# A transformer block on one core: the exponentials of softmax shared between ScalarE and VectorE

## The chip, the cores and the metric

The kernel runs on one core of a Trainium2 chip. The metric is device time in microseconds (us) of one execution. The engines are named as the profile names them: PE (TensorE matmuls), PEld (its weight loads), ACT (ScalarE), DVE (VectorE), POOL (GpSimd) and SP (SyncE, which here issues the DMAs). "Clock" is the mean clock that the throttle granted to TensorE, as a share of full speed. All runs whose times are compared here were in the same (fast) state.

## The reference

One layernorm feeds an attention block and a feed-forward block; both are added to the input. S = 2048 tokens, D = 512, 32 heads of 16 elements, F = 1792, bf16 inputs.

```python
# cut to what matters; shapes reshaped and transposed in the original
def reference(A_x, A_wqkv, A_wo, B_x, B_w1, B_w3, B_w2):
    xn = _layernorm(A_x)
    # A: attention
    q, k, v = split_heads(xn @ wqkv)                 # 32 heads, Dh = 16
    scores = einsum("bhqd,bhkd->bhqk", q, k) * (16 ** -0.5)
    o = einsum("bhqk,bhkd->bhqd", softmax(scores), v) @ wo
    # B: SwiGLU
    h = silu(xn @ w1) * (xn @ w3)
    return A_x + o + h @ w2
```

There are 32 x 2048 x 2048 exponentials, 134 million. They come as 2048 score tiles of 128 keys x 512 queries.

## The kernel before

The kernel is planned while it is built. A small planner walks through time with estimated durations, gives each engine a fixed order of instructions, and turns every "this reads what that wrote" into a semaphore wait. That order is fixed when the program is built, so the estimates decide the order and the chip decides the time.

```python
NU = NQC * NG          # 32 units: 4 blocks of 512 queries x 8 groups of 4 heads
RPU = 4 * NT           # 64 score tiles per unit
NR = NU * RPU          # 2048 score tiles
GW = 3                 # score tiles per exp
...
a_cost = lambda n: 0.113 + 0.000835 * n      # what the planner thinks ScalarE needs
d_cost = lambda n: 0.095 + 0.00104 * n       # and VectorE
```

Three score tiles go into three PSUM banks, and one ScalarE instruction takes the exponential of all three (128x1536). There are two such buffers (banks 0 to 2 and 3 to 5), bank 6 is for all dense work (projections and feed-forward), bank 7 for the sum over keys.

```python
def try_score():
    ...                                       # a free one of the two buffers, or return False
    for i, r in enumerate(rs):                # rs: three score tiles
        b = 3 * buf + i
        mms.append((b, KT[32 * j:32 * j + 32, g, kt * 128:(kt + 1) * 128],
                    QT[32 * j:32 * j + 32, u % 3, :], 32 * j))
    o = P.op("pe", f, reads=rd, writes=wr, dur=0.30, name="S%d" % n)
    ...
    def emit():
        q = P.op("act", lambda e: e.activation(
            PT[:, s0:s0 + w, :].rearrange("p a b -> p (a b)"), ps[:, 3 * buf * 512:(3 * buf + w) * 512],
            ACTF.Exp, scale=SCALE),
            reads=wr, writes=[("PT", r % NSL) for r in rs], dur=a_cost(512 * w))
        ...

def try_pv():                                 # four heads at once, each in its own columns of the array
    ...
    for j in range(4):
        ins = e.matmul(bank(PV)[32 * j:32 * j + 17, :], Vaug[:, kt, 4 * g + j, :],
                       PT[:, (4 * m + j) % NSL, :], start=(kt == 0), stop=(kt == NT - 1),
                       tile_position=(0, 32 * j))
```

The 17th column of `Vaug` is all ones, so the same matmul also gives the denominator of the softmax. A head has 16 elements but stands on 32 rows; the K and Q weights are padded with zeros to that width, so half of each K and Q projection computes zeros:

```python
wk = wko[:, :].rearrange("p (a b) -> p a b", b=32)     # 16 weights, 16 zeros per head
...
elif try_score() or try_pv() or try_dense():           # PE's priorities in the planner
    moved = True
```

## Time and profile before

| | before |
|---|---|
| median time, 3 runs | 1023.9 us (1023.38 to 1024.24) |
| busy: ACT, PE, DVE | 94%, 79%, 20% |
| mean granted clock | 0.824 |
| exps | 683 (all but one of 128x1536), starting every 1.33 us (median) |

First, lines from the profile's page: the span; busy time of each engine in us, as a share of the span, and its instructions; the granted clock in 40 equal slices (9 is 90% or more); the chain of work that ended last, by engine; and the costliest group of instructions (busy us, mean ns of one, then the engine's idle time just before them and what ended most of it).

```profile
span 1022.1 us, 19380 instructions
...
PE 803.3 (79%) x8641; PEld 221.6 (22%) x8641; DVE 203.1 (20%) x347; ACT 959.1 (94%) x755; POOL 61.0 (6%) x81
...
PEclk9999999975579999855559999955558999975578
...
ACT 77%; PE 15%; DVE 3%; DMA 2%; issue 2%; SPq 0%; DVEq 0%
...
L1464 ACT ACTIVATE f_PT<-ps 128x1536 bf16<-128x1536 f32 (+1 forms) x683 | 940.6, 1661 | 24.2 <-PE ps L1454 24.0
```

ScalarE bounds the kernel. It works 94% of the time, the chain runs through it, and before all 683 exps together it waited only 24 us. VectorE is nearly idle: that is what the change wants to use.

One exp lasts 1661 ns, but 683 of them take less time than 683 x 1.66 us would be, because the end of one overlaps the start of the next. The timeline shows it (start, duration, engine, line, operation, how many in a row, and the idle time before):

```profile
457.73 13.68 ACT L1464 ACTIVATE f_PT<-ps 128x1536 bf16<-128x1536 f32 x10
...
464.75 0.61 PE L1454 MATMUL ps<-f_QT,f_KT 32*128 32x512 bf16 x3 [0.20 <-ACT f_PT L1464]
...
466.10 0.61 PE L1454 MATMUL ps<-f_QT,f_KT 32*128 32x512 bf16 x3 [0.20 <-ACT f_PT L1464]
```

Ten exps in 13.68 us: taking one duration off leaves nine distances, (13.68 - 1.66) / 9 = 1.34 us each. This distance from start to start, here called the pitch, and not the duration, is what an exp costs a busy ScalarE. PE's score groups follow in the same step of 1.35 us, each released by an exp.

The table by windows gives, for two stretches: length, busy us (instructions) of PE, PEld, DVE, ACT and POOL, granted clock, DMA share and GB/s.

```profile
150.00:200.00 50.00, 40.44 (x521) 11.90 (x510) 14.93 (x23) 49.19 (x41) 1.26 (x1) 1.00 0.25 30
450.00:500.00 50.00, 37.83 (x244) 7.51 (x248) 2.58 (x5) 49.19 (x37) 1.27 (x1) 0.53 0.16 6
```

ACT is full in both. In the second there is no feed-forward work left for this block of queries, PE runs 244 matmuls in place of 521, and the clock falls to 0.53. PE still looks 76% busy there, because each matmul lasts longer (0.59 us on average, against 0.38 us in the first stretch). Fewer matmuls and a lower clock stand together here; what sets the clock is not shown.

Finally, one line of the groups by form, which matters later: the 16 normalisations of the layernorm on VectorE.

```profile
L1096 DVE TENSOR_SCALAR f_xn_sb<-f_x_sb,f_lnr,f_lnb 128x512 bf16<-128x512 bf16 x16 | 9.4, 630 | 1.2 <-PE ps L1214 0.9 <-POOL f_lnb L1084 0.3
```

### The profile page before, as it was taken

Reading aid. Unit: us, or ns where it says so; the run is one execution under the profiler, and the core shown is the slowest. Engines: PE = TensorE matmul, PEld = TensorE weight load, DVE = VectorE, ACT = ScalarE, POOL = GpSimd, SP = SyncE. Lnnn points to the kernel's source line nnn. Section 1 sums busy time; section 2 is a strip of 40 time slices with the busy share of each in tenths; the row PEclk is TensorE's granted clock in tenths of the full one; section 3 lists DMA queues with packets and bytes.
Section 4 is the critical chain, followed back from the end, with each engine's and each line's share of the span. In section 5 each row is a group of like instructions: output and inputs, shape, how many; then the busy total and the mean of one; then the engine's idle time right before and its main releaser. Section 6 shows DMA issues by size and latency. Waiting matters only on the chain.

```text
span 1022.1 us, 19380 instructions
## 1 busy us (share of the span) xinstructions
PE 803.3 (79%) x8641; PEld 221.6 (22%) x8641; DVE 203.1 (20%) x347; ACT 959.1 (94%) x755; POOL 61.0 (6%) x81
## 2 busy tenths in 40 slices
PE   4987878777799777777789877777779977777795
PEld 2322222221122222111113222211112222211122
DVE  7742233310001222100001222200001122210012
ACT  2799999999999999999999999999999999999991
POOL 5200000000000000000000000000000000000000
PEclk9999999975579999855559999955558999975578
DMA  5402222210111332111111133211101233201112
GB/s 170 89 12 38 38 35 36 22 6 2 6 12 18 58 48 42 23 6 6 6 6 18 35 55 48 38 6 7 5 3 12 38 48 48 33 3 5 6 7 31
DMA packets 80173, 28.88 MB, mean 28 GB/s; under 512 B 70096, under 2 KB 78032, under 8 KB 80080
## 3 DMA queue, kind: packets, MB, share of 16 engines
q1 hardware_dynamic: 80080, 27.54, 21.5%
q8 instruction: 70, 1.15, 0.5%
q14 instruction: 23, 0.19, 0.1%
HBM read 20.71 MB, written 2.10 MB: 22 GB/s over the span
## 4 chain that ended last, share of the span: by engine, by line
ACT 77%; PE 15%; DVE 3%; DMA 2%; issue 2%; SPq 0%; DVEq 0%
ACT f_PT L1464 74%; PE ps L1192 9%; PE ps L1454 4%; ACT f_th L1291 3%; PE ps L1491 2%; DMA f_wv<-in_A_wqkv_dram 1%; DVE f_KT L1203 1%; DMA f_Lc<-f_U 1%; DVE f_hT L1305 0%; DMA f_R<-f_Rrow 0%; DVE f_xn_sb L1096 0%; DVE f_t L1295 0%; PE ps L1214 0%; DVE f_QT L1203 0%; DVE f_osb L1352 0%
## 5 line engine op out<-in xcount | busy, mean ns | idle before, releaser
L1464 ACT ACTIVATE f_PT<-ps 128x1536 bf16<-128x1536 f32 (+1 forms) x683 | 940.6, 1661 | 24.2 <-PE ps L1454 24.0
L1454 PE MATMUL ps<-f_QT,f_KT 32*128 32x512 bf16 x2048 | 319.6, 462 | 139.5 <-ACT f_PT L1464 136.1
L1491 PE MATMUL ps<-f_PT,f_Vaug 128*17 128x512 bf16 x2048 | 239.7, 459 | 0.7 <-DVE f_U L1508 0.7
L1454 PEld LDWEIGHTS ps<-f_QT,f_KT 32*128 32x128 bf16 x2048 | 68.6, 94 | 434.8 <-ACT f_PT L1464 387.9
L1192 PE MATMUL ps<-f_xnT,f_w 128*32 128x512 bf16 x1792 | 129.3, 381 | 38.8 <-DVE f_t L1295 26.6
L1544 POOL TENSOR_TENSOR f_onorm<-f_U,f_R 128x512 bf16<-128x512 f32 x31 | 39.4, 1270 | 908.3 <-DMA f_R<-f_Rrow 749.1
L1491 PEld LDWEIGHTS ps<-f_PT,f_Vaug 128*17 128x17 bf16 x2048 | 50.1, 88 | 156.6 <-issue 148.6
L1508 DVE COPY f_U<-ps 128x512 f32<-128x512 f32 x32 | 22.1, 691 | 241.1 <-PE ps L1491 240.8
L1192 PE MATMUL ps<-f_w,f_hT 128*32 128x512 bf16 x896 | 64.8, 398 | 2.8 <-DVE f_osb L1352 1.6
L1295 DVE SCALAR_TENSOR_TENSOR f_t<-f_th,ps 128x512 f32<-128x512 f32 x56 | 38.5, 687 | 135.2 <-ACT f_th L1291 134.8
L1192 PEld LDWEIGHTS ps<-f_xnT,f_w 128*32 128x32 bf16 x1792 | 42.7, 95 | 86.9 <-issue 61.2
L1305 DVE SCALAR_TENSOR_TENSOR f_hT<-f_t,ps 128x512 bf16<-128x512 f32 x56 | 38.5, 687 | 93.8 <-PE ps L1192 93.8
L1192 PE MATMUL ps<-f_xnT,f_wq 128*32 128x512 bf16 x512 | 47.0, 484 | 7.2 <-DVE f_t L1295 5.6
L1291 ACT ACTIVATE f_th<-ps 128x512 f32<-128x512 f32 x56 | 49.2, 878 | 1.4 <-PE ps L1192 1.4
L1203 DVE CAST f_QT<-ps 128x512 bf16<-128x512 f32 x32 | 22.1, 691 | 127.5 <-PE ps L1192 127.4
L1192 PE MATMUL ps<-f_xnT,f_wko 128*32 128x512 bf16 x512 | 36.5, 389 | 4.7 <-DVE f_t L1295 2.5
L1192 PE MATMUL ps<-f_wo,f_onorm 128*32 128x512 bf16 x512 | 36.7, 388 | 3.5 <-DVE f_onorm L1544 3.5
L1203 DVE CAST f_KT<-ps 128x512 bf16<-128x512 f32 x32 | 22.1, 690 | 45.5 <-PE ps L1192 45.5
L1192 PEld LDWEIGHTS ps<-f_w,f_hT 128*32 128x32 bf16 x896 | 22.3, 98 | 26.8 <-issue 6.6
L1352 DVE TENSOR_TENSOR f_osb<-ps,f_x_sb 128x512 bf16<-128x512 f32 x12 | 8.3, 690 | 84.7 <-PE ps L1192 84.7
L1192 PE MATMUL ps<-f_wv,f_xnT 128*32 128x512 bf16 x256 | 19.7, 443 | 3.8 <-DMA f_wv<-in_A_wqkv_dram 3.5
L1223 ACT ACTIVATE f_xnT<-ps 128x512 bf16<-128x512 bf16 x14 | 7.6, 605 | 15.0 <-PE ps L1214 15.0
(46 smaller groups left out, 137.6 us busy)
## 6 DMA issues: line engine op xcount, KB each, us to landing
f_w<-in_B_w_dram SPq DMA_DIRECT2D x112, 128.0 KB
f_R<-f_Rrow SPq DMA_DIRECT2D x128, 32.0 KB
out_dram<-f_osb SPq DMA_DIRECT2D x16, 128.0 KB
f_w<-in_B_w_dram SPq DMA_DIRECT2D x1, 1792.0 KB
f_x_sb<-in_A_x_dram SPq DMA_DIRECT2D x3, 512.0 KB
f_hT<-in_A_wqkv_dram SPq DMA_DIRECT2D x2, 512.0 KB
f_x_sb<-in_A_x_dram SPq DMA_DIRECT2D x2, 256.0 KB
f_wv<-in_A_wqkv_dram SPq DMA_DIRECT2D x1, 512.0 KB
```

What stands on the lines that cost most here:

```text
L1192: ins = e.matmul(bank(bk)[32 * i:32 * i + 32, 0:ncols], make_lhsT(i), rhs_ap, start=start, stop=stop, tile_position=(0, 32 * i))
L1203: q = P.op("dve", lambda e: e.tensor_copy(dst, src_fn(bk)), reads=[("ps", bk)], writes=[key], dur=d_cost(n))
L1223: q = P.op("act", lambda e: e.activation(xnT[:, :, t * 128:(t + 1) * 128], tb, ACTF.Identity), reads=[("ps", bk)], writes=[("xnT", t)], du ...
L1291: q = P.op("act", lambda e: e.activation(th[:, ss, :], bank(bk), ACTF.Tanh, scale=0.5), reads=[("ps", bk)], writes=[("th", ss)], dur=a_cos ...
L1295: q2 = P.op("dve", lambda e: e.scalar_tensor_tensor(t1[:, ss, :], th[:, ss, :], 1.0, bank(bk), ALU.add, ALU.mult), reads=[("th", ss), ("ps ...
L1305: q = P.op("dve", lambda e: e.scalar_tensor_tensor(hT[:, fc, :], t1[:, ss, :], 0.5, bank(bk), ALU.mult, ALU.mult), reads=[("t1", ss), ("ps ...
L1352: q = P.op("dve", lambda e: e.tensor_tensor(osb[:, ts, :], bank(bk), other, ALU.add), reads=[("ps", bk), ("osum", ts) if part == 2 else (" ...
L1454: ins = e.matmul(bank(b), l_, r_, start=True, stop=True, tile_position=(rp, 0))
L1464: q = P.op("act", lambda e: e.activation(PT[:, s0:s0 + w, :].rearrange("p a b -> p (a b)"), ps[:, 3 * buf * 512:(3 * buf + w) * 512], ACTF ...
L1491: ins = e.matmul(bank(PV)[32 * j:32 * j + 17, :], Vaug[:, kt, 4 * g + j, :], PT[:, (4 * m + j) % NSL, :], start=(kt == 0), stop=(kt == NT ...
L1508: q = P.op("dve", lambda e: e.tensor_copy(U[:, us, :], bank(PV)), reads=[("ps", PV)], writes=[("U", us)], dur=d_cost(512))
L1544: q = P.op(eng, lambda e: e.tensor_tensor(onorm[:, g, :], U[:, us, :], R[:, :], ALU.mult), reads=[("U", us)] + [("R", j_) for j_ in range( ...
```

## The change

The intent is to give part of the exponentials to VectorE, where they are made not by one exp instruction but by arithmetic on bit patterns. The score in PSUM is scaled (through Q) to y = 128 * (s / ln 2 + 127). As a 16-bit integer, y is the bit pattern of a bf16 number: its high bits are the exponent of 2^(s/ln 2), its low seven bits the fraction f. Three bf16 numbers are made from it by 16-bit operations: E = 2^e (the fraction masked away); L * M, where L is the pattern itself, 2^e (1+f), and M = (1+f)/2; and a "shifted chord", the pattern minus 352. Their sum is proportional to 2^(e+f) to about 0.1% (worked out from the formula in the code). The sum is never formed on VectorE: the three terms go through the PV matmul one after another, and PSUM adds them. So a VectorE pair costs PE three times the PV matmuls.

What else changes:

- The exps are pairs (128x1024, two banks) in place of triples: ScalarE has two buffers, banks 0-1 and 2-3, VectorE has banks 4-5.
- The offset 127*128 is added by the score matmul itself: one row of KT holds the constant, the same row of QT holds ones. ScalarE has to take it off again, with a per-partition bias tensor, `act_bias`.
- K and Q heads are no longer padded in the weights. The projection computes two head groups at once, VectorE copies it to a staging tile, and four DMAs per group place the heads on their 32-row strips. Half of the K and Q matmuls fall away.
- The constant rows of KT are filled before the start: two of eight groups on ScalarE, six on GpSimd.
- The buffer of the VectorE terms (`xd`) lies over the tile of x. Its outputs carry the write keys of x, and x is loaded again at the end.

```diff
-    GW = 3
-    NGR = (NR + GW - 1) // GW
-    NSL = 24
+    NPR = 10
+    NON = 11
+    ND = 3
+    YB = 127.0 * 128.0
+    QS = SCALE * 128.0 / math.log(2.0)
+    ASC = math.log(2.0) / 128.0
...
+            e.memset(act_bias[:, :], -127.0 * math.log(2.0) + math.log(KAPPA))
...
+        for g in range(2, NG):
+            P.post("pool", lambda g=g: done.__setitem__(("KTi", g), P.op("pool", lambda e: e.tensor_scalar(
+                KT[:, g, :], sel1[:, 0:1].to_broadcast((128, S)), YB, None, ALU.mult),
+                reads=[("sel1",)], writes=[("KT", g, i) for i in range(NQC)], dur=2.5).end), ready=9.0 + g, prio=3)
...
+                def moves(hh):
+                    for j in range(4):
+                        m = P.dma(lambda e, j=j: e.dma_start(dst(hh)[32 * j:32 * j + 16, :],
+                                                             stg[64 * hh + 16 * j:64 * hh + 16 * j + 16, sl, :]),
...
+                q = P.op("act", lambda e: e.activation(PT[:, s_, :], ps[:, b0 * 512:(b0 + 2) * 512], ACTF.Exp,
+                                                       scale=ASC, bias=act_bias[:, 0:1]),
+                         reads=[("ps", b0), ("ps", b0 + 1), ("abias",)], writes=[("PT", s_)], dur=a_cost(1024))
...
+                q = P.op("dve", lambda e: e.tensor_scalar(yb[:, ys, :], ps[:, 4 * 512:6 * 512], 0.0, 32767.0,
+                                                          ALU.max, ALU.min),
+                         reads=[("ps", 4), ("ps", 5)], writes=[("yb", ys)], dur=1.24)
...
+                def f_e():
+                    q_ = P.op("dve", lambda e: e.tensor_scalar(dsl[:, s_, 0, :], yb[:, ys, :], 0x7F80, None,
+                                                               ALU.bitwise_and),
+                              reads=[("yb", ys)], writes=[("ds", s_, 0)] + XD, dur=0.34)
+                    give(0, q_)
+                def f_m():
+                    P.op("dve", lambda e: e.tensor_scalar(mb[:, ys, :], yb[:, ys, :], 0x7F, 0x3F00,
+                                                          ALU.bitwise_and, ALU.bitwise_or),
+                         reads=[("yb", ys)], writes=[("mb", ys)], dur=0.34)
+                def f_g():
+                    q_ = P.op("dve", lambda e: e.tensor_scalar(dsl[:, s_, 1, :], yb[:, ys, :], -352.0, 0.0,
+                                                               ALU.add, ALU.max),
+                              reads=[("yb", ys)], writes=[("ds", s_, 1)] + XD, dur=0.34)
+                    give(1, q_)
+                def f_t():
+                    q_ = P.op("dve", lambda e: e.tensor_tensor(dsl[:, s_, 2, :].bitcast(BF16),
+                                                               yb[:, ys, :].bitcast(BF16), mb[:, ys, :].bitcast(BF16),
+                                                               ALU.mult),
+                              reads=[("yb", ys), ("mb", ys)], writes=[("ds", s_, 2)] + XD, dur=0.62)
+                    give(2, q_)
...
-                    elif try_score() or try_pv() or try_dense():
+                    elif try_a() or try_d() or try_pv() or try_dense():
```

## The prediction

It was written before the changed kernel had been built or run.

> **What bounds the kernel now.** ScalarE. The busy table has ACT at 959.1 of 1022.1 us (94%), PE 79%, VectorE (DVE) 20%; the chain of waits is 74% ACT exps. In the timeline without feed-forward work (459–471 us), exps of 128x1536 start every 1.345 us though one lasts 1.66 us; a 512-wide tanh costs a pitch of 0.48 us. So a pitch is about 0.06 us + 0.85 ns per column, and 683 exps plus 56 tanhs make about 945 us. The rest is start (about 45 us) and tail. In stages without feed-forward work its granted clock is 0.50–0.57, elsewhere 1.00 (table by windows). [...] the slow windows are those with only 120–130 matmuls per 25 us, against 240 or more.
>
> **What changes.** 1024 pairs (128x1024) replace 683 triples. A pair on ACT should have a pitch of 0.91 us (from the fit). A pair on DVE takes five operations:
> - clamp from PSUM: 128x512 lasts 0.69 us, so 1024 lasts about 1.22;
> - three 16-bit tensor-scalars. [...] The trace's 64-element bf16 ones, 0.174 us alone, 0.09 us pitch, [...];
> - one 16-bit multiply, [...].
>
> Outputs share one set of write keys, so two also wait for the operation before. I estimate 3.1 us per pair; the plan's own table assumes 2.88.
>
> The order is fixed at build time. With its table it balances at about 210 pairs on DVE (190–235).
> - ACT: 814 x 0.91 + 27 = about 770 us.
> - DVE: 210 x 3.1 = 650, plus about 165 of old work (203 now, less half of the K and Q copies) = about 820 us, 90% of the span, from 20%.
> - PE: 256 K and 256 Q matmuls fall away; each DVE pair adds four PV matmuls (about 840); score groups rise from 683 to 1024. At full clock in the timeline a group of four takes 0.22 us; scores to PV and back cost about 0.1 us extra each way (0.32 and 0.31 between starts). So: about 0.4 x 814 + 60 (scores) + 0.22 x 740 (PV) + 0.22 x 992 (dense) = about 770 us.
>
> Removed from the critical path: about 175 us of ACT. Returned: engines stand at 770–820 us of a span near 850, in one fixed order, with only two score buffers for ACT (1.23 + 0.4 us of a 1.83 us round trip, so a PE queue delay over 0.15 us stalls ACT), a DVE running about 8% slower than planned and a start lengthened slightly by packing DMAs. I add about 55 us.
>
> **Predicted: 905 us, range 845 to 975.** Faster by over 2%: 0.93; within 2%: 0.04; slower: 0.03.
>
> **What would show it.** ACT exps 128x1024, about 810, pitch 0.91–1.05 us, ACT busy about 85%; about 210 DVE clamps of 1.2 us; DVE about 90% busy and large in the chain of waits, with PE; [...] granted clock mostly 1.0, mean above 0.92[...]; exps waiting for PE scores for 50–100 us in total against 24 now.
>
> **What would make it wrong.** [...] PE staying at half clock outside feed-forward stages, so that PE bounds (over 950 us); [...] or the fixed order absorbing delays better than I think (850–870 us).

Passages that no trace of this case shows are cut out of it, and the cuts are marked. The prediction put a VectorE pair at 3.1 us, of which the clamp is 1.22. The 3.1, and the 820 us for VectorE made from it, stay as the author's estimate. It can be followed from the planner's durations in the diff (1.24 + 3 x 0.34 + 0.62 = 2.88) and about 0.1 us for each of the two waits.

## The result, and the profile after

The changed kernel takes 969.5 us (median of 4 runs, 966.89 to 971.24) against 1023.64 us (4 runs) for the kernel before. Ratios here and below are the mean time of one kernel's fast runs over that of the other's of the same rounds, so they are not quite the ratios of the quoted medians. This one is 0.9477, 95% interval 0.9444 to 0.951. The change saves 54 us; the prediction said 119. The time lies in the predicted range, near its slow end, but only 54 of the expected 119 us came.

From the page of the kernel after, the lines that answer those of before, and the five operations of a VectorE pair:

```profile
span 968.4 us, 21733 instructions
...
PE 858.6 (89%) x9033; PEld 240.4 (25%) x9033; DVE 878.7 (91%) x1437; ACT 853.9 (88%) x872; POOL 91.4 (9%) x82
...
PEclk9779799999989999999999999999999999999988
...
ACT 43%; DVE 33%; PE 17%; issue 2%; DMA 2%; SPq 2%; DVEq 0%
...
L1550 ACT ACTIVATE f_PT<-ps,f_act_bias 128x1024 bf16<-128x1024 f32 x798 | 819.1, 1153 | 51.3 <-PE ps L1513 44.1
...
L1593 DVE TENSOR_SCALAR f_yb<-ps 128x1024 int16<-128x1024 f32 x226 | 274.4, 1214 | 5.3 <-PE ps L1513 4.9
...
L1627 DVE TENSOR_TENSOR f_xd<-f_yb,f_mb 128x1024 bf16<-128x1024 bf16 x226 | 159.5, 706 | 8.9
...
L1616 DVE TENSOR_SCALAR f_mb<-f_yb 128x1024 int16<-128x1024 int16 x226 | 100.8, 446 | 5.1
L1621 DVE TENSOR_SCALAR f_xd<-f_yb 128x1024 int16<-128x1024 int16 x226 | 98.9, 438 | 7.1
L1610 DVE TENSOR_SCALAR f_xd<-f_yb 128x1024 int16<-128x1024 int16 x226 | 101.3, 448 | 0.0
...
L1134 DVE TENSOR_SCALAR f_xn_sb<-f_xd,f_lnr,f_lnb 128x512 bf16<-128x512 bf16 x16 | 35.3, 2244 | 0.3 <-POOL f_lnb L1122 0.3
```

The planner gave 226 of the 1024 pairs to VectorE. The five operations add up to 274.4 + 159.5 + 100.8 + 98.9 + 101.3 = 734.9 us, 3.25 us per pair if durations are added (one can begin before the last has ended). The clamp that reads PSUM costs 1.21 us; the 16-bit operations are faster, 0.44 us (one input) and 0.71 us (the multiply of two) for the same 1024 elements. The clock is at full speed almost everywhere (mean 0.964). Between 450 and 500 us it is 1.00 with 480 matmuls, where before it was 0.53 with 244; the longest gap between matmuls is as long in both (0.94 and 0.95 us), so that gap does not tell the clock here. And now three engines stand at 88 to 91%, with the chain divided among them. One line stands out: the 16 normalisations take 35.3 us, against 9.4 us before.

Where did the time go? I cut each trace at two points: the start of the exp after the first 2% of all exps (a clamp of VectorE counts as one), and the end of ScalarE's last exp.

| part of the span, us | before | after | difference |
|---|---|---|---|
| start, until 2% of the exps | 54.8 | 81.0 | +26 |
| middle, until the last exp ends | 945.8 | 845.5 | -100 |
| tail | 21.5 | 41.9 | +20 |
| span | 1022.1 | 968.4 | -54 |

So the middle gained 100 us, and nearly half of that was given back at the two ends. The timeline of the kernel after shows each end, and the middle:

```profile
26.77 10.73 POOL L1158 TENSOR_SCALAR f_KT<-f_sel 128x2048 bf16<-128x2048 f32 x2
26.82 10.83 DVE L1134 TENSOR_SCALAR f_xn_sb<-f_xd,f_lnr,f_lnb 128x512 bf16<-128x512 bf16 x2
...
539.29 8.19 ACT L1550 ACTIVATE f_PT<-ps,f_act_bias 128x1024 bf16<-128x1024 f32 x8
...
925.34 1.19 ACT L1550 ACTIVATE f_PT<-ps,f_act_bias 128x1024 bf16<-128x1024 f32 x1
...
931.53 7.57 PE L1216 MATMUL ps<-f_xnT,f_w 128*32 128x512 bf16 x96
...
938.93 3.19 PE L1216 MATMUL ps<-f_w,f_hT 128*32 128x512 bf16 x56
```

- Start: two of GpSimd's fills run from 26.77 to 37.50 us, and two normalisations on VectorE start right after and end with them, at 37.65. Undisturbed, one lasts 0.41 us.
- Middle: eight exps in 8.19 us. Taking off one duration of 1.15, seven distances of 1.006 us remain, not the 0.91 us that the prediction had. The median pitch over the whole trace is 0.997 us.
- Tail: the last exp starts at 925.34, and then PE runs dense matmuls: 469 matmuls start after the last exp ends (336 of the feed-forward, 128 of the attention's output projection), against 177 before (100 and 72).

The middle and the tail as rows of the table by windows:

```profile
75.00:926.00 851.00, 785.27 (x8090) 210.81 (x8082) 803.29 (x1338) 823.02 (x838) 41.63 (x31) 0.98 0.24 31
926.60:968.40 41.80, 28.90 (x469) 12.54 (x469) 12.40 (x24) 1.79 (x3) 0.00 (x0) 0.86 0.20 36
```

and the tail before:

```profile
1000.60:1022.10 21.50, 11.04 (x181) 4.63 (x177) 6.14 (x15) 0.00 (x0) 0.00 (x0) 0.79 0.27 37
```

In the 851 us of the middle ACT is busy 97%, DVE 94% and PE 92%. There is little idle time anywhere, but these shares alone do not tell which engine sets the time. The clamps of VectorE start every 3.78 us on average, at best (the shortest tenth) every 3.12 us.

### The profile page after: what moved, and what is told of

The parts are those of the page before. It is cut to its first block, busy times and chain, and to the rows that moved or that the text cites. A ratio compares the mean times of both kernels' runs of the same rounds, so it can differ in the third digit from the quotient of the medians.

```text
span 968.4 us, 21733 instructions
## 1 busy us (share of the span) xinstructions
PE 858.6 (89%) x9033; PEld 240.4 (25%) x9033; DVE 878.7 (91%) x1437; ACT 853.9 (88%) x872; POOL 91.4 (9%) x82
## 4 chain that ended last, share of the span: by engine, by line
ACT 43%; DVE 33%; PE 17%; issue 2%; DMA 2%; SPq 2%; DVEq 0%
ACT f_PT L1550 42%; DVE f_yb L1593 9%; PE ps L1216 8%; PE ps L1513 5%; DVE f_xd L1627 4%; PE ps L1673 4%; DVE f_xd L1610 3%; DVE f_xd L1621 3%; DVE f_mb L1616 3%; DVE f_xn_sb L1134 3%; DVE f_t L1350 2%; ACT f_th L1346 2%; SPq L1283 1%; DVE f_hT L1360 1%; DMA f_wkv<-in_A_wqkv_dram 1%
## 5 line engine op out<-in xcount | busy, mean ns | idle before, releaser
L1550 ACT ACTIVATE f_PT<-ps,f_act_bias 128x1024 bf16<-128x1024 f32 x798 | 819.1, 1153 | 51.3 <-PE ps L1513 44.1
L1593 DVE TENSOR_SCALAR f_yb<-ps 128x1024 int16<-128x1024 f32 x226 | 274.4, 1214 | 5.3 <-PE ps L1513 4.9
L1673 PE MATMUL ps<-f_xd,f_Vaug 128*17 128x512 bf16 x1356 | 238.7, 388 | 4.5 <-DVE f_xd L1610 2.9
L1216 PE MATMUL ps<-f_xnT,f_w 128*32 128x512 bf16 x1792 | 169.7, 396 | 19.4 <-DVE f_t L1350 13.8
L1627 DVE TENSOR_TENSOR f_xd<-f_yb,f_mb 128x1024 bf16<-128x1024 bf16 x226 | 159.5, 706 | 8.9
L1616 DVE TENSOR_SCALAR f_mb<-f_yb 128x1024 int16<-128x1024 int16 x226 | 100.8, 446 | 5.1
L1621 DVE TENSOR_SCALAR f_xd<-f_yb 128x1024 int16<-128x1024 int16 x226 | 98.9, 438 | 7.1
L1610 DVE TENSOR_SCALAR f_xd<-f_yb 128x1024 int16<-128x1024 int16 x226 | 101.3, 448 | 0.0
L1673 PEld LDWEIGHTS ps<-f_xd,f_Vaug 128*17 128x17 bf16 x1356 | 57.1, 89 | 69.6 <-issue 29.3
L1350 DVE SCALAR_TENSOR_TENSOR f_t<-f_th,ps 128x512 bf16<-128x512 f32 x56 | 38.1, 680 | 7.4 <-ACT f_th L1346 6.8
L1360 DVE SCALAR_TENSOR_TENSOR f_hT<-f_t,ps 128x512 bf16<-128x512 bf16 x56 | 38.1, 681 | 4.1 <-PE ps L1216 2.6
L1134 DVE TENSOR_SCALAR f_xn_sb<-f_xd,f_lnr,f_lnb 128x512 bf16<-128x512 bf16 x16 | 35.3, 2244 | 0.3 <-POOL f_lnb L1122 0.3
```

The source lines that it names most:

```text
L1134: o = P.op("dve", lambda e: e.tensor_scalar(xn_sb[:, xs, :], x_sb[:, t, :], lnr[:, t:t + 1], lnb[:, t:t + 1], ALU.mult, ALU.add), reads=[( ...
L1216: ins = e.matmul(bank(bk)[32 * i:32 * i + 32, 0:ncols], make_lhsT(i), rhs_ap, start=start, stop=stop, tile_position=(0, 32 * i))
L1350: q2 = P.op("dve", lambda e: e.scalar_tensor_tensor(t1[:, ss, :], th[:, ss, :], 1.0, bank(bk), ALU.add, ALU.mult), reads=[("th", ss), ("ps ...
L1550: q = P.op("act", lambda e: e.activation(PT[:, s_, :], ps[:, b0 * 512:(b0 + 2) * 512], ACTF.Exp, scale=ASC, bias=act_bias[:, 0:1]), reads= ...
L1593: q = P.op("dve", lambda e: e.tensor_scalar(yb[:, ys, :], ps[:, 4 * 512:6 * 512], 0.0, 32767.0, ALU.max, ALU.min), reads=[("ps", 4), ("ps" ...
L1610: q_ = P.op("dve", lambda e: e.tensor_scalar(dsl[:, s_, 0, :], yb[:, ys, :], 0x7F80, None, ALU.bitwise_and), reads=[("yb", ys)], writes=[( ...
```

## The experiments

The theories after the result:

- **A**: ScalarE still bounds the middle, so its pitch per pair decides. Against the fit, one exp costs 0.09 us too much; the candidates for that were the bias tensor, the two-level form, the buffers, or a wrong fit.
- **B**: VectorE bounds the middle: 3.78 us per pair times 226 is the 850 us, and ScalarE only waits its turn.
- Beside these, the start is lengthened by GpSimd against VectorE, and PE is short of time because each VectorE pair triples its PV work.

Up to `e8`, the edits are against the kernel after. Differences between experiments are differences of medians, partly from different chips; the kernel before, run beside each of them, had medians of 1022 to 1024 us.

### micro_exp: the pitch of an exp by itself

The kernel does nothing but exps from PSUM (a wrong result), six in a row of each kind.

```python
for w, t in zip(WIDTHS, plain):          # 512 ... 2048 columns
    for r in range(REPS):
        e.activation(t[:, r * w:(r + 1) * w], ps[:, 0:w], ACTF.Exp, scale=0.25)
for r in range(REPS):                    # the same 1024 columns with a bias tensor
    e.activation(bia[:, r * 1024:(r + 1) * 1024], ps[:, 0:1024], ACTF.Exp, scale=0.25, bias=bias[:, 0:1])
# then: alternating bank pairs (alt), and a two-level access pattern (lev)
```

> Wrong result on purpose: no attention, only exps from PSUM on ScalarE, six back to back of each width (512, 768, 896, 1024, 1152, 1280, 1536, 2048 columns), then 1024 columns with a bias tensor, over two bank pairs in turn, and with a two-level pattern. Theory A (pitch is linear in the width, 0.06 us + 0.85 ns per column, as I fitted for the prediction; the 1.005 us pitch in the kernel after is then a wait for PE): start to start 0.48, 0.71, 0.82, 0.91, 1.04, 1.15, 1.345, 1.78 us. Rival B (a 1024-wide exp itself costs 1.005 us, by its shape): 1.00 us for 1024 here too, with no other engine running, and some of the other widths off the line as well. Rival C (the bias tensor costs it): 0.91 without and 1.00 with bias.

| 128 x columns | 512 | 768 | 1024 | 1280 | 1536 | 2048 | 1024 with bias tensor | 1024 alternating banks | 1024 two-level |
|---|---|---|---|---|---|---|---|---|---|
| pitch, us | 0.477 | 0.691 | 0.904 | 1.118 | 1.331 | 1.758 | 0.997 | 0.904 | 0.904 |

The timeline of this kernel, six exps per line:

```profile
53.80 6.68 ACT L54 ACTIVATE bias<-ps,bias 128x1024 bf16<-128x1024 f32 x6
59.78 6.20 ACT L58 ACTIVATE alt<-ps 128x1024 bf16<-128x1024 f32 x6
65.21 6.27 ACT L60 ACTIVATE lev<-ps 128x1024 bf16<-128x1024 f32 x6
```

The first group stands 5.98 us ahead of the second, the second 5.43 us ahead of the third: 0.997 and 0.904 us per exp. The pitch without a bias tensor is 0.051 us + 0.833 ns per column, so the prediction's fit was right, for that form. The bias tensor adds 0.093 us to every exp, and 0.997 is exactly the median pitch of the kernel after. In 798 exps that is 74 us of ScalarE's time. The before kernel had no such operand in its exps, the diff adds one, and the prediction had no term for it.

### e1_fill_act: GpSimd's fills moved to ScalarE

```diff
-            P.post("pool", lambda g=g: done.__setitem__(("KTi", g), P.op("pool", lambda e: e.tensor_scalar(
-                KT[:, g, :], sel1[:, 0:1].to_broadcast((128, S)), YB, None, ALU.mult),
-                ... dur=2.5).end), ready=9.0 + g, prio=3)
+            P.post("act", lambda g=g: done.__setitem__(("KTi", g), P.op("act", lambda e: e.activation(
+                KT[:, g, :], sel1[:, 0:1].to_broadcast((128, S)), ACTF.Identity, scale=YB),
+                ... dur=1.9).end), ready=9.0 + g, prio=3)
```

> The six constant fills of K on GpSimd (5.4 us each in the trace of after) move to ScalarE (1.9 us each), nothing else. Theory: they hold up the normalisations on VectorE (35 us for 16, against 9 us before), and so delay the first steady exps from about 50 to about 75 us. Then the normalisations fall to about 9-12 us, the first clamp on VectorE comes at about 50 us instead of 73, and the time falls by 18-25 us to about 948 us. Rival: the start is long because K and Q now go through a staging tile and DMAs (about 2 us each to land) and because of the single score buffer; then normalisations get shorter but the first clamp stays after 65 us and the time falls by less than 8 us.

Measured: 950.0 us, ratio to before 0.9282 (0.9244 to 0.9321), 19.5 us faster than the kernel after. Groups by form:

```profile
L1134 DVE TENSOR_SCALAR f_xn_sb<-f_xd,f_lnr,f_lnb 128x512 bf16<-128x512 bf16 x16 | 9.4, 631 | 1.0 <-POOL f_lnb L1122 1.0
...
L1158 ACT ACTIVATE f_KT<-f_sel 128x2048 bf16<-128x2048 f32 x6 | 11.2, 1908 | 0.0
```

The normalisations are back at 9.4 us, the first clamp starts at 54.8 us, where it had started at 73.1, and the start by the cut above is 63.3 us (was 81.0). The theory of the start is confirmed for most of it; the start is still 8.5 us longer than before (54.8 us), for which the packing DMAs are a candidate that was not tested. In the trace of the kernel after, two normalisations lasted as long as two fills of 5.37 us (10.83 and 10.73 us). That the fills hold the normalisations up is shown by this run; by what mechanism is not.

### e2_no_d: the new form without VectorE's share

```diff
         def try_d():
             r0 = st["pos"]
-            if r0 >= NR or st["early"] or not idle((4, 5)) or dbuf[0] > P.t:
-                return False
+            return False
```

> VectorE gets no exps; pairs, packing, score buffers as after. Shows what the rest of the change costs before the sharing pays. Theory (exps bound by ScalarE at 1.005 us a pair where three banks cost 1.345 us before): 1024 x 1.005 + 27 + start about 70 + tail 20 = about 1140 us, 11% slower than before, mean granted clock under 0.9 again. Rival (the pitch of 1.005 us comes from PE load or bank conflicts with the VectorE stream): without that stream the pitch falls to about 0.91 us and the time is about 1050 us.

Measured: 1293.42 us, ratio 1.2652 (1.26 to 1.2704), clock 0.716. All 1024 pairs on ScalarE are much slower than either kernel, and slower than expected. One window of it:

```profile
600.00:650.00 50.00, 36.32 (x186) 6.82 (x184) 1.79 (x4) 44.23 (x42) 1.26 (x1) 0.53 0.14 8
```

In 50 us ScalarE gets only 42 instructions through, at clock 0.53; in the timeline two exps start per 2.36 us, 1.18 us each. PE runs 186 matmuls there, and a group of scores lasts 0.61 us, where in the kernel after it takes 0.39 at clock 1.00. Over the run ScalarE waits 139 us before its exps, 96 of them for PV matmuls. As I read it, a PV group stands before the next scores in the fixed order, and two buffers of two banks give ScalarE too little slack for matmuls that long. That the new form by itself (pairs, bias, packing, and only two banks in each of ScalarE's buffers) loses 26% is measured; which of its parts does is not. The sharing wins that back, and more: 1293 to 969.5 us.

### e3_split512: each exp of 1024 as two of 512

```diff
+                def two(e):
+                    for i in range(2):
+                        ins = e.activation(PT[:, s_, 512 * i:512 * i + 512], ps[:, (b0 + i) * 512:(b0 + i + 1) * 512],
+                                           ACTF.Exp, scale=ASC, bias=act_bias[:, 0:1])
+                    return ins
```

> Each exp of 1024 columns on ScalarE is issued as two of 512, one after the other, same plan and order. If 512 columns have a pitch of 0.48 us (as the tanhs do), a pair costs 0.96 instead of 1.005 us, 36 us less ScalarE work: if ScalarE binds the steady stage, 15-35 us faster than after (935-955 us); if VectorE and PE bind it, the time stays within 6 us of after. If the pitch of a pair was a wait for PE, the sum of both halves stays at 1.005 us and nothing changes.

Measured: 1060.01 us, ratio 1.0373 (1.0336 to 1.0411). The halves have a pitch of 0.569 us, 1.14 us per pair, where I had expected 0.48 each. The miss has the same cause as the main one: 0.477 from the table plus 0.093 for the bias is 0.570. The expectation was written before the result of the micro benchmark, which ran in the same series. As ScalarE then has 84% of the chain of waits and the time rises by 90 us, ScalarE's pitch does set the time once it is long enough.

### e4_no_bias: the offset moved to the clamp

Without the constant row the score is 128 s / ln 2, ScalarE needs no bias, and VectorE's clamp, one instruction with two operations, adds the offset itself. The upper clamp is given up; the result was still correct.

```diff
-    YB = 127.0 * 128.0
+    YB = 0.0
+    YD = 127.0 * 128.0 + 128.0 * math.log2(D_SCALE)
...
-                                                       scale=ASC, bias=act_bias[:, 0:1]),
+                                                       scale=ASC),
...
-                q = P.op("dve", lambda e: e.tensor_scalar(yb[:, ys, :], ps[:, 4 * 512:6 * 512], 0.0, 32767.0,
-                                                          ALU.max, ALU.min),
+                q = P.op("dve", lambda e: e.tensor_scalar(yb[:, ys, :], ps[:, 4 * 512:6 * 512], YD, 0.0,
+                                                          ALU.add, ALU.max),
```

> The offset of the bit-pattern exps moves from the K rows and ScalarE's bias tensor into the clamp on VectorE (add, then max, in place of max and min), so that the exps on ScalarE need no bias tensor; plan, order and counts stay those of after. The exp's pitch should fall from 1.005 to 0.91 us where it runs back to back (the measurement of exps alone gave 0.997 with and 0.904 without), so ScalarE has about 74 us less work. Theory A (ScalarE binds the steady stage in after): 35-70 us faster than after, about 900-935 us. Theory B (VectorE and PE, in the fixed order, bind it): 0-20 us faster, ScalarE busy falls to about 80% and its waits for PE grow by what it saves.

Measured: 958.58 us, ratio 0.9376 (0.9342 to 0.941): 11 us faster, though ScalarE lost 47 us of busy time. From the page:

```profile
DVE 68%; PE 19%; issue 5%; DMA 3%; ACT 2%; SPq 2%; DVEq 0%
...
L1551 ACT ACTIVATE f_PT<-ps 128x1024 bf16<-128x1024 f32 x798 | 769.5, 1029 | 83.2 <-PE ps L1514 57.1
```

The shorter exp became a longer wait (83.2 us before the exps, was 51.3), and the chain went from ACT 43% to DVE 68%. For this edit alone theory B holds: behind ScalarE stood VectorE.

### e5_xd: VectorE's outputs without the keys of x

Only the first use of each of the three term buffers has to wait for x; later uses carry the keys of x for nothing. With those keys, an output also waits for the completion of the output before it: in the kernel after, VectorE stood idle for 7.1 and 8.9 us in all before two of the three (lines L1621 and L1627 above).

```diff
-                              reads=[("yb", ys)], writes=[("ds", s_, 0)] + XD, dur=0.34)
+                              reads=[("yb", ys)], writes=[("ds", s_, 0)] + (XD if nd < ND else []), dur=0.34)
```

(The same in the two other outputs.)

> From the fourth VectorE pair on, the three outputs no longer share write keys with the x tile, so that each operation need not wait for the one before to complete. Per pair 3.25 us of busy time should fall to about 2.95-3.05 (two waits of about 0.1 us less), 45-60 us less VectorE work in total. If VectorE binds the steady stage: 20-40 us faster than after. If ScalarE (1.005 us per pair) or PE binds: under 8 us.

Measured: 956.3 us, ratio 0.935 (0.9317 to 0.9384), 13 us faster. The shortest tenth of the clamp's pitch falls from 3.12 to 2.87 us, which is the sum of the planner's own durations (2.88). That is neither of the two expectations (20 to 40 us, or under 8). The two waits are gone, as the page shows, and the chain turns the other way:

```profile
L1627 DVE TENSOR_TENSOR f_xd<-f_yb,f_mb 128x1024 bf16<-128x1024 bf16 x226 | 156.8, 694 | 0.1
...
L1621 DVE TENSOR_SCALAR f_xd<-f_yb 128x1024 int16<-128x1024 int16 x226 | 98.6, 436 | 0.0
...
ACT 69%; PE 13%; DVE 12%; SPq 2%; DMA 2%; issue 1%; DVEq 0%
```

So make VectorE faster and ScalarE is the limit; make ScalarE faster and VectorE is.

### e6_half_d: fewer pairs on VectorE

```diff
             st["dpar"] ^= 2
+            st["dpos"] = r0 + 14
```

> VectorE gets 143 pairs instead of 226, at least seven pairs apart; else as after. ScalarE then has 881 exps. If ScalarE's pitch of 1.005 us binds: 83 more exps are 83 us, partly given back in start and tail: about 1030-1050 us, 6-8% slower than after. If VectorE or PE (83 x 4 fewer PV matmuls, 83 fewer tile-mode switches) bind after, it is not more than 3% slower than after (under 1000 us).

A "tile-mode switch" here is the step from a score group to another group of matmuls and back. In the kernel after, at clock 1.00 (474 to 477 us), a score group and its neighbours start 0.31 to 0.33 us apart, dense and PV groups 0.22 to 0.24.

Measured: 1075.04 us, ratio 1.0533 (1.0475 to 1.0591), clock 0.857, 143 pairs on VectorE and 881 on ScalarE. It is slower than even theory A expected; that the clock fell with the PV work (0.857, against 0.964 in the kernel after) fits this, but was not tested by itself. By this run the planner's share of 226 was not too high.

### e7_three: the three edits together

`e7` is `e1`, `e4` and `e5` in one kernel.

> The three edits together: constant fills on ScalarE, no bias tensor, separate write keys. If the savings add, ScalarE ends at 730+65 us of work and VectorE at about 800, and the time is about 880 us. If PE with its fixed order is the next limit (I estimate about 810 us of PE time with mode switches, plus start and tail), it stays at 905-930 us.

Measured: 912.62 us (909.47 to 913.85), ratio to before 0.8913 (0.8877 to 0.895), and the result is correct. This is the fastest version: 10.9% faster than the kernel before, and 57 us faster than the kernel after. The single savings add up to only 19.5 + 11 + 13 = 43.5 us. From its page:

```profile
PE 836.2 (92%) x9033; PEld 236.2 (26%) x9033; DVE 817.3 (90%) x1437; ACT 810.3 (89%) x878; POOL 59.1 (6%) x76
...
PE 49%; DVE 29%; ACT 14%; DMA 2%; SPq 2%; issue 2%; POOL 0%; DVEq 0%
```

The pitch of the exps is 0.921 us (median), that of the clamps 3.61 us (mean). PE now has the largest part of the chain.

### e8_one_term: a third of the PV work for VectorE's pairs

Its output is wrong, which doesn't matter for the time. Two of the three terms are computed but never summed. If PE's extra work is what limits the kernel after, this must show.

```diff
-                left = [6]
+                left = [2]
...
                               reads=[("yb", ys)], writes=[("ds", s_, 0)] + XD, dur=0.34)
-                    give(0, q_)
```

(The same for `give(1, q_)`, and the counts of tasks per unit.)

> Wrong result on purpose: from after, a VectorE pair still does all five operations, but only one of its three terms goes into the PV matmuls, which takes away 223 x 4 matmuls (about 50 us of PE time at 0.22 us a group, more with mode switches). If PE's queue holds back the exps and the dense work in after: 35-60 us faster (910-935 us), fewer matmuls after the last exp. If ScalarE (1.0 us pitch) and VectorE alone set the pace: 5-20 us faster, from the tail only.

Measured: 969.78 us, ratio 0.9485 (0.9451 to 0.9519), clock 0.898 (0.964 in the kernel after): the same time as the kernel after. Both expectations missed. Two things cancel: the tail takes 25 us (263 matmuls) in place of 42 us (469), but the last exp ends 11 us later, at 937.9 in place of 926.5 us. The windows show where the middle lost; first the kernel after, for comparison:

```profile
450.00:500.00 50.00, 46.06 (x480) 12.57 (x478) 48.51 (x80) 49.51 (x52) 2.73 (x2) 1.00 0.30 39
```

then `e8`, with its tail in the last row:

```profile
450.00:500.00 50.00, 43.62 (x376) 10.84 (x376) 44.50 (x73) 45.97 (x48) 2.94 (x2) 0.84 0.26 31
500.00:550.00 50.00, 48.16 (x416) 11.42 (x416) 44.76 (x75) 48.31 (x48) 1.27 (x1) 0.75 0.12 15
937.90:963.10 25.20, 14.94 (x265) 6.96 (x263) 6.68 (x15) 0.00 (x0) 0.00 (x0) 0.84 0.27 43
```

PE has a fifth fewer matmuls in the first window and is hardly less busy, while the granted clock falls to 0.84 and 0.75, and VectorE and ScalarE get less done there (73 and 48 instructions, were 80 and 52). So it looks as if part of what is saved in matmuls is lost in clock. That the clock held up the exps is argued, not shown: with fewer PV tasks the planner also made another order (223 pairs on VectorE). In sum, the extra PV work of the three terms costs no time here.

### e12, e13, e14: what was still open after e7

`e12` is `e7` without the moved fills, to see why three edits gave more than their sum.

```diff
# e12: against e4
-                              reads=[("yb", ys)], writes=[("ds", s_, 0)] + XD, dur=0.34)
+                              reads=[("yb", ys)], writes=[("ds", s_, 0)] + (XD if nd < ND else []), dur=0.34)
```

> After with the edits of e4 (no bias tensor) and e5 (separate write keys), without the constant fills of e1. If the two relieve independent waits their gains add: 11 + 13 = 24 us, about 945 us. If ScalarE and VectorE take turns as the limit, so that each alone uncovers the other, the gain is larger than the sum: 35-42 us, 928-935 us (e7 less the 20 us of the start).

Measured: 932.67 us, ratio 0.9121 (0.9087 to 0.9154). Bias and keys together save 37 us, apart 11 + 13 = 24. That is the mark of two engines which take turns as the limit: each edit alone only uncovers the other engine. The fills add another 20 us (932.67 to 912.62), the same as alone (19.5), since the start is a stage of its own.

`e13` repeats `e8` on top of `e7`, since PE's part of the chain is larger there. Its output is wrong, which doesn't matter for the time.

```diff
# e13: against e7
-                left = [6]
+                left = [2]
... (give(0, q_), give(1, q_) and the counts as in e8)
```

> Wrong result on purpose: e7 with one PV term per VectorE pair instead of three (as e8 was from after). If PE's added PV work binds e7: 25-50 us faster, 865-890 us. If it does not, or if PE's clock falls with the lighter load as in e8 (0.90 against 0.96): 900-920 us.

Measured: 917.7 us, ratio 0.8983 (0.8954 to 0.9013), clock 0.909 (`e7`: 0.973). No gain again, and for the same two reasons: the tail is 25 us in place of 42, and the last exp ends 20 us later (889.5 us, 869.4 in `e7`). The windows, `e7` first:

```profile
450.00:500.00 50.00, 47.93 (x518) 13.23 (x520) 48.60 (x89) 49.45 (x56) 2.54 (x2) 1.00 0.29 39
```

and `e13`:

```profile
450.00:500.00 50.00, 46.80 (x372) 10.99 (x368) 46.17 (x80) 46.73 (x51) 2.77 (x2) 0.76 0.19 15
```

Even where the chain names PE most often, a kernel with 28% fewer matmuls in this window is not faster.

`e14` gives VectorE more pairs, by telling the planner that ScalarE is slower than it is.

```diff
# e14: against e7
-        a_cost = lambda n: 0.113 + 0.000835 * n
+        a_cost = lambda n: 0.19 + 0.000835 * n
```

> The three edits of e7, and the plan takes an exp pair on ScalarE as 1.045 us instead of 0.968, so that VectorE gets 239 pairs instead of 226 and fewer dense groups (about 73 instead of 119 PE operations in the plan) stand behind the last exp. If dense work in the leftover PE slots is what runs out of time, the tail shortens by about 15 us and the exps end later by about as much: 905-920 us. If VectorE at 226 pairs was already the limit: over 920 us.

Measured: 943.18 us, ratio 0.9201 (0.9164 to 0.9238), 239 pairs on VectorE. The last exp ends at 921.1 us (869.4 in `e7`), though the tail is only 25 us; DVE has 49% of the chain. The clamps keep their mean distance (3.62 us, 3.61 in `e7`), so 13 more of them make up 47 of the 52 us by which the exps end later. This fits a VectorE that was already at its limit with 226 pairs.

### e9, e10, e11: attempts on the tail

In `e7` 469 matmuls, the same as in the kernel after, still wait when the last exp is done, and the tail is 42 us. Three edits of the plan tried to get them done earlier.

```diff
# e9: against e7
-                    elif try_a() or try_d() or try_pv() or try_dense():
+                    elif try_a() or try_dense() or try_d() or try_pv():
```

> The three edits of e7, and dense groups go ahead of VectorE's scores and PV in the plan. VectorE then gets 202 pairs instead of 226, and only about 40 matmul groups stand behind the last exp instead of about 117. If the tail of 42 us is dense work pushed behind the exps, it falls to about 21 us, while 24 more exps cost about 24 us: no gain, 905-935 us. If the tail is the softmax end chain, it stays near 40 us and the time rises to 930-945 us.

Measured: 1012.46 us, ratio 0.9931 (0.987 to 0.9993), clock 0.909. The tail did shrink to 28 us (145 matmuls), but the last exp ended at 982.0 us. The waits of ScalarE (total us, times, longest):

```profile
ACT f_PT L1551 <- PE ps L1514: 60.6, 57, 10.1
ACT f_PT L1551 <- PE ps L1674: 56.0, 38, 11.2
```

In `e7` these two are 30.4 and 8.6 us, with longest waits of 5.3 and 0.6. Waits of 10 us are not a queue of a few matmuls; SP's issues of the packing DMAs have 6% of the chain.

```diff
# e10: against e9, planner durations set to measured ones
-        a_cost = lambda n: 0.113 + 0.000835 * n
+        a_cost = lambda n: 0.06 + 0.000835 * n
-            x = score(2 * buf, "A", 0.27)
+            x = score(2 * buf, "A", 0.41)
... (VectorE's scores 0.1 or 0.41, PV 0.23, dense group 0.22)
```

> As e9, and the plan's own durations are set to measured ones: exp pitch 0.06 us + 0.835 ns per column, score pair 0.41 us of PE with its switches, PV group 0.23, dense group 0.22. VectorE gets 190 pairs. If the fixed order from wrong durations costs time: 885-900 us. If PE, ScalarE and VectorE are simply full, 905-930 us.

Measured: 1000.57 us, ratio 0.9796 (0.9744 to 0.9848). It missed as well; the packing DMAs' issues have 7 to 8% of the chain. That one queue of DMA issues in fixed order blocks Q and K behind other waits fits both, but it was not tested.

```diff
# e11: against e7
-        a_cost = lambda n: 0.113 + 0.000835 * n
+        a_cost = lambda n: 0.06 + 0.000835 * n
```

> The three edits of e7, and only the plan's duration of an exp is set to the measured one (0.915 us for a pair instead of 0.968). VectorE gets 214 pairs. If the share of exps was wrong for the faster ScalarE: 890-905 us. If PE binds e7 (its chain of waits is 49% PE): within 6 us of e7 (907-918 us).

Measured: 940.27 us, ratio 0.9206 (0.9168 to 0.9244), 214 pairs on VectorE. With ScalarE's true cost in the plan, the exps finish 14 us earlier than in `e7` (855.2 us), but 671 matmuls are left and the tail is 82 us. So the exps cannot simply be hurried: this plan leaves more dense work over. None of the three expectations was met.

## Why the prediction was right or wrong

Right were the mechanism and most of its terms:

- The direction, and how the work is shared: about 210 pairs on VectorE (226), about 810 exps on ScalarE (798).
- VectorE's operations: clamps 1.2 us (1.21), VectorE at 90% (91%) and large in the chain (33%). A pair with its waits was put at 3.1 us; the shortest tenth of the distances between clamps is 3.12 us. That the 90% came out is luck: VectorE's work was put at 820 us and is 879 us, of a longer span. Of this, 26 us are the normalisations held up at the start, and 16 more pairs than expected cost about 50 us by the prediction's own 3.1.
- The clock above 0.92 on average (0.964), and the exps' wait for PE's scores of 50 to 100 us (51.3 us, of which 44.1 for scores).

Wrong was the size of the gain, 54 us in place of 119. The terms that failed, as the prediction put them (the first three; the fourth is there to read `e7` rightly):

1. **"A pair on ACT should have a pitch of 0.91 us (from the fit)."** The fit is right for an exp without a bias tensor (0.904 us), but the diff adds one to every exp: 0.997 us (`micro_exp`). "ACT: 814 x 0.91 + 27 = about 770 us" should have been about 814 x 0.997 + 27 = 839; the trace has ACT busy 823 us of the 851 us in the middle. So the step "Removed from the critical path: about 175 us of ACT" failed: ACT's busy time fell by 105 us (959.1 to 853.9). Taken away, this cost is worth 11 us alone (`e4`) and 24 us once the write keys are gone (`e12` against `e5`, 956.3 - 932.67).
2. **"A start lengthened slightly by packing DMAs."** The start grew by 26 us, and the packing DMAs were not the main cause. GpSimd's fills of KT held up VectorE's normalisations, 35.3 us against 9.4; moving the fills gave 19.5 us back (`e1`), and 8.5 us of the longer start remain. I had named GpSimd as a risk, but only its later multiplies.
3. **The tail**, for which the prediction had no term. I took it to stay as it was; it grew by 20 us (469 matmuls left against 177). In the plan the exps outrun the dense work, which runs only where PE has nothing better to do. How much is left is fixed with the order: seven kernels with the same plan (after, `e1`, `e3`, `e4`, `e5`, `e7`, `e12`) all have 469 matmuls left and a tail of 41 to 43 us, however fast their exps are. Another plan moves it: 263 matmuls and 25 us with a third of the PV work (`e8`, `e13`), 671 and 82 us with a shorter exp in the plan (`e11`). The prediction's PE sum of about 770 us was also low, by the profile's measure: PE is busy for 859 us.
4. **VectorE's shared write keys.** These were seen and rightly costed ("two also wait for the operation before"), so they are no part of the miss. Taking them away is a gain that the prediction had not counted: 13 us alone (`e5`), and 37 us together with the bias (`e12`).

The middle as a whole was not far off: 905 us less the start and tail of before (54.8 and 21.5) leaves 829 us, and it took 845.5. About three quarters of the miss of 64 us lay at the ends (26 and 20 us). By this arithmetic the 55 us that the prediction allowed for friction covered most of the mis-sized pitch, which is luck. `e7`, the kernel with the pitch (0.921) and most of the start that the prediction assumed, takes 912.6 us, near the predicted 905; but its tail is still 42 us, and it gains by the missing keys, which the prediction had not counted on. For the kernel after with only the bias and the fills mended I estimate 958.6 - 19.5 = 939 us, from `e4` and `e1`; that kernel was not run. So those two terms are about 30 us of the miss by experiment, the tail is 20 us by the trace, and the rest is not assigned.

Theory A and theory B are both half right. The chain of waits names ScalarE (43%) and VectorE (33%), and `e4`, `e5` and `e12` show that they take turns. Saving on the tripled PV work brought no time as it was tried, twice (`e8`, `e13`): the tail became 17 us shorter and the exps ended 11 and 20 us later, at a lower clock.

Open stays how to shorten the tail without a loss elsewhere, and what exactly delayed the exps in `e9` and `e10`. The DMA issue queue is suspected from the chain, not shown.

## What to carry to other kernels

When work moves between engines, cost the exact form of each new instruction, operand by operand: a bias that comes as a tensor in place of a constant cost 10% of every exp here. Follow the change into the start and the tail too, since a bounded middle that gets faster leaves both exposed: here they took 46 of 100 us back. And when two engines are both near their limit, judge fixes together, not one at a time, because each alone only uncovers the other (11 and 13 us apart, 37 together).
